# Softmax normalisation of a fused attention and two-MLP kernel: GpSimd keeps the tiles of 320 to 448 keys, DVE and ACT take the others

## The chip, the cores and the metric

One core of a Trainium2 chip runs the kernel. The time is that of the whole launch on the device in microseconds (us), the median of three runs. The engines are PE (TensorE: matrix products and transposes), DVE (VectorE), ACT (ScalarE), POOL (GpSimd) and SP, whose queue issues nearly all DMAs.

## The reference

Causal attention, a gated MLP and an MLP with a rational function follow each other, all in float32:

```python
def _attn_ref(q, k, v):                 # q, k, v: 2 x 12 x 448 x 64
    scores = scale * np.matmul(q, k.transpose(0, 1, 3, 2))
    mask = np.triu(np.ones((seq, seq), dtype=bool), k=1)
    scores = np.where(mask, -1000000000.0, scores)
    scores = scores - np.max(scores, axis=-1, keepdims=True)
    attn = np.exp(scores)
    attn = attn / (np.sum(attn, axis=-1, keepdims=True) + 1e-09)
    return np.matmul(attn, v).astype(np.float32)
...
def _moe_ref(x, w_in, w_out):           # 896 x 768, 768 x 2048, 2048 x 768
    h = x @ w_in
    relu6 = np.clip(h + 3.0, 0.0, 6.0)
    g = h * relu6 / 6.0
    return (g @ w_out).astype(np.float32)
...
def _moe2_ref(x, w_in, w_out, a, b):    # same shapes, g = P(h) / (Q(h) + 1e-6)
```

## The kernel before

The work has two stages. The attention stage takes the 24 heads in 12 pairs, numbered 0 to 11. A pair has seven tiles, r = 0 to 6: 64 queries of each of its two heads against (r + 1) * 64 keys, so tiles of 64 to 448 keys. For each pair PE forms the scores (`a_scores`, L427), DVE adds the mask and takes the row maximum (`a_max`, L439), ACT takes the exponential and its row sums (`a_exp`, L446). In two parts (tiles 6, 5, 0, then 4, 3, 2, 1) the sums get 1e-9 added on ACT or DVE (`a_bias`) and DVE takes the reciprocals (`a_recip`, L462). Then every tile of exponentials is multiplied by its reciprocals: `a_norm`, the normalisation, on GpSimd in this kernel (L470). PE transposes the tiles in four groups (`a_transpose`, L476; the first two groups hold tiles 5, 6 and 0), ACT or DVE moves each group from PSUM to SBUF (`a_move`, tiles `et`, L326 on ACT and L328 on DVE), PE multiplies with v (`a_apply`, L496), and ACT and DVE split the result into a high and a low part (`xh`, L326, and `xl`, L508). The buffers of the exponentials (`e0` to `e6`) exist twice, so pair n + 2 waits for pair n.

The MLP stage follows: 2304 matmuls of 448 columns (L715). Their weights come as float64, are loaded in chunks and are rebuilt by ACT (`full`, `tail`, high part, L610, L616, L326) and DVE (L620, L626, low part, L644). The first chunks are prepared, and the first products formed, while the attention stage still runs.

No engine picks its work at run time. The class `Program` writes out each engine's queue when the kernel is built: it plays the operations through a list of costs, and where two operations could start at the same time it takes the one with the smaller due time. The due time is the operation's place (pair number times `PAIR`) plus an offset for its kind in `DUE`. Where an operation names several engines with a cost each, the planner takes the engine on which it starts first. Each engine then works through its queue strictly in order. `STAY` holds PE back from switching between groups of operations. These numbers are planning figures and not measured ones.

Of the kernel before, what the change touches and what calls it, by code (L numbers as in the profile page):

```python
# [35 lines left out]
class Program:  # L36
# [15 lines left out]

    TILING = {"scores": "quarters", "apply": "columns"}
    DRAIN = 0.16
    STAY = 5.83

    def __init__(self, rings, banks, due):
        self.rings, self.banks, self.due = rings, banks, due
# [2 lines left out]
    def add(self, kind, at, engines, fn, *args, reads=(), writes=(), new=()):  # L61

        self.ops.append((kind, at, engines, fn, args, tuple(reads), tuple(writes), tuple(new)))

    def order(self):
# [44 lines left out]
        while can:  # L112
            best = None
            for n, t in can.items():
# [20 lines left out]
                for e, cost in ops[n][2].items():  # L135
                    mine = max(t[e], free[e], room), due[n] + self.STAY * turn, n, e, cost
                    if best is None or mine < best:
# [46 lines left out]
def c_act(n):  # L184
    return 0.051 + n / 1200


def c_dve(n):
    return 0.068 + n / 960


def c_pool(n):
    return 0.15 + n * 0.0021


def c_pe(n, passes):
    return passes * (0.0025 + n / 2400)

# [5 lines left out]
def c_mm(n, passes):  # L204
# [2 lines left out]


DUE = {
    "load": -89.1,  # L210
    "keep": 0.0,
    "fetch": -20.0,
    "load v": -0.1,
    "norm": 4.2,
    "scores": 10.5,
    "max": -10.7,
    "exp": 31.3,
    "bias": 13.8,
    "reciprocal": -27.8,
    "transpose": -38.3,  # L220
    "move": 7.4,
    "apply": 15.3,
    "x hi": -25.6,
    "x rest": 70.4,
    "constants": -8.8,
    "w load": -84.1,
    "magnitude": -7.3,
    "tail": -30.5,
    "shift": 17.2,
    "sign": -12.6,  # L230
    "w hi": 79.6,
    "w rest": -29.6,
    "product": 0.0,
    "relu": 8.8,
    "gate": 1.1,
# [17 lines left out]
    "out": -3.6,  # L253
    "store": 7.5,
}
PAIR = 5.9


def plan(KM, KF):
# [17 lines left out]
def tile_attention_moe_moe2(  # L277
# [235 lines left out]
    for n in range(len(pairs)):  # L513
        t, last = PAIR * n, n == len(pairs) - 1
        for which in ("kr", "qr"):
            raw = which, n
            add(
                "load", t, {"act" if n == 0 and which == "qr" else "dma": 1.26}, qk_load, which, n,
                writes=[raw], new=[(which, raw)],
            )  # L520
        add(
            "load v", t, {"dma": 0.9}, v_load, n, reads=[("empty", n % VB)], writes=[("v", n)],
            new=[("v", ("v", n))],
        )
        sc = [("sc", n, held) for held in BANKS]
        add(
            "scores", t, {"pe": 1.7}, a_scores, n, reads=[("kr", n), ("qr", n)],
            writes=sc + ["scored"] * last, new=[("s", key) for key in sc],
        )
        for late, r in enumerate(order):  # L530
            w, first, mine = (r + 1) * CP, late == 0, next(held for held in BANKS if r in held)
            add(
                "max", t + late, {"dve": c_dve(w)}, a_max, n, r,
                reads=[("sc", n, mine), "masks"] + [("stat", n)] * (not first)
                + [("m", n, mine[0])] * (r != mine[0]),
                writes=[("e", n, r), ("st", n, r), ("m", n, r)] + [("stat", n)] * first,
                new=[(f"e{r}", ("e", n, r))] + [("stat", ("stat", n))] * first,
            )
            add(
                "exp", t + late, {"act": 0.235 + c_act(w)}, a_exp, n, r, reads=[("stat", n)],  # L540
                writes=[("e", n, r), ("st", n, r)],
            )
        for part, held in enumerate((STRAIGHT, SWAPPED)):
            add(
                "bias", t + 2 * part, {"act": 0.2, "dve": 0.1}, a_bias, n, part,
                reads=[("st", n, r) for r in held] + [("stat", n)], writes=[("r", n, part)],
            )
            add(
                "reciprocal", t + 2 * part, {"dve": 0.15}, a_recip, n, part, reads=[("stat", n)],
                writes=[("r", n, part)],  # L550
            )
            for r in held:
                w = (r + 1) * CP
                add(
                    "norm", t + 2 * part, {"pool": c_pool(w)}, a_norm, n, r,
                    reads=[("r", n, part), ("stat", n)], writes=[("e", n, r)],
                )
        for g, group in enumerate(GROUPS):
            add(
                "transpose", t + g, {"pe": 0.436}, a_transpose, n, g,  # L560
                reads=["masks", ("pads", n % EB)] + [("e", n, r) for r in sorted({r for r, _ in group})],
                writes=[("pt", n, g)], new=[("t", ("pt", n, g))],
            )
            add(
                "move", t + g, {"act": c_act(512), "dve": c_dve(512)}, a_move, n, g,
                reads=[("pt", n, g)], writes=[("et", n, g)], new=[("et", ("et", n, g))],
            )
        for a, gs_ in enumerate(APPLY):
            cols = 1024 * len(gs_) // len(GROUPS)
            add(  # L570
                "apply", t + 2 * a, {"pe": c_pe(cols, 4) + 0.1}, a_apply, n, a,
                reads=[("et", n, g) for g in gs_] + [("v", n)], writes=[("o", n)],
                new=[("o", ("o", n))] if a == 0 else (),
            )
        b, hp = pairs[n]
        add("x hi", t, {"act": c_act(S) + 0.04}, a_hi, n, reads=[("o", n)], writes=[("x", hp, b)])
        add("x rest", t, {"dve": c_dve(S)}, a_lo, n, reads=[("o", n)], writes=[("x", hp, b)])
# [22 lines left out]
    raw, full, tail, split = {}, {}, {}, {}  # L600
# [54 lines left out]

    base = PAIR * len(pairs) + 10

# [208 lines left out]
    t, i, every = base, 0, tuple(range(B))  # L866
# [6 lines left out]
    while i < len(chunks):  # L873

        side = chunks[i][0][0] == 2
        n = 1 if not side else 2 if chunks[i + 2][0][0] == 2 else 3
# [72 lines left out]
```

## Time and profile before

| | |
|---|---|
| median of 3 runs (lowest to highest) | 560.67 us (560.19 to 560.80) |
| the profiled execution: its own time / its span | 560.22 / 558.4 us |
| busy: PE, DVE, ACT, POOL | 538.7, 423.2, 397.9, 82.2 us |
| chain that ended last, by line | 82% MLP matmuls (L715), 11% GpSimd's normalisation (L470) |
| mean granted TensorE clock | 0.991 |

The span goes from the first to the last instruction in the trace; the run's own time holds a little more. Busy time is that in which an engine has an instruction in work. The chain is followed back from the last instruction, at each step to what released it.

### The profile page before, as it was taken

How to read it: one execution, taken by the hardware profiler on the slowest of the kernel's cores; microseconds unless marked ns; L12 is line 12 of the kernel's file. 1: busy time of each engine (PE TensorE's matmuls, PEld its weight loads, DVE VectorE, ACT ScalarE, POOL GpSimd, SP SyncE). 2: the span in 40 equal slices, each digit the busy share in tenths (PEclk: the TensorE clock that was granted, in tenths of full speed). 3: DMA queues.
4: the chain of work that ended last, by engine and by line, in shares of the span. 5: the costliest groups of instructions: out<-in, count | busy, mean ns of one | idle time of the engine just before them, and what ended most of it. 6: DMA issues, size and time to landing. Idle time of an engine off the chain costs nothing.

```text
span 558.4 us, 9410 instructions
## 1 busy us (share of the span) xinstructions
PE 538.7 (96%) x3236; PEld 492.8 (88%) x3236; DVE 423.2 (76%) x925; ACT 397.9 (71%) x882; POOL 82.2 (15%) x104
## 2 busy tenths in 40 slices
PE   6888887999999999999999999999999999999997
PEld 5766766999999999999999999999999999999996
DVE  3588784679999998777777349999989999975420
ACT  5798885579898987776776359788678778855410
POOL 3999978000000000000000000000000000000000
PEclk9699999999999999999999999999999999999999
DMA  5775141147778777777766342234324323336100
GB/s 163 219 202 166 43 119 58 54 146 213 249 253 242 258 231 279 258 252 242 243 236 223 136 137 85 86 94 165 110 85 136 118 86 103 124 112 188 61 33 33
DMA packets 39311, 87.12 MB, mean 156 GB/s; under 512 B 4704, under 2 KB 14688, under 8 KB 39264
## 3 DMA queue, kind: packets, MB, share of 16 engines
q1 hardware_dynamic: 39104, 86.30, 47.9%
q8 instruction: 25, 0.41, 0.3%
q10 hardware_dynamic: 160, 0.23, 0.1%
q14 instruction: 22, 0.18, 0.1%
HBM read 71.18 MB, written 15.34 MB: 155 GB/s over the span
## 4 chain that ended last, share of the span: by engine, by line
PE 85%; POOL 11%; DVE 2%; issue 1%; ACT 1%; POOLq 0%; DVEq 0%
PE bank L715 82%; POOL e L470 11%; DVE e L439 1%; PE bank L476 1%; PE bank L376 1%; PE bank L496 1%; PE bank L427 1%; ACT et L326 0%; DVE et L328 0%; POOLq L945 0%; ACT e L446 0%; ACT o L326 0%; DVE stat L462 0%; ACT tail L616 0%; POOL ident masks.py:199 0%
## 5 line engine op out<-in xcount | busy, mean ns | idle before, releaser
L715 PE MATMUL bank<-yh,w 128*128 128x448 f32 x384 | 112.0, 362 | 0.0
L715 PE MATMUL bank<-rh,w 128*128 128x448 f32 x384 | 97.2, 362 | 0.0
L715 PE MATMUL bank<-xh,w 128*128 128x448 f32 x384 | 93.7, 363 | 0.0
L715 PE MATMUL bank<-ph,w 128*128 128x448 f32 x384 | 92.6, 362 | 0.0
L644 DVE TENSOR_TENSOR w<-full,w 128x384 fp32r<-128x384 f32 x96 | 53.2, 555 | 46.0 <-ACT w L326 45.6
L326 ACT ACTIVATE w<-full 128x384 fp32r<-128x384 f32 x96 | 50.2, 523 | 51.6 <-PE bank L715 50.8
L616 ACT ACTIVATE tail<-raw 128x384 uint32<-128x384 uint8 x128 | 69.4, 554 | 23.0 <-DVE full L620 19.7
L610 ACT ACTIVATE full<-raw 128x384 f32<-128x384 f32 x128 | 68.9, 549 | 20.2 <-DVE w L644 19.1
L620 DVE SCALAR_TENSOR_TENSOR full<-full,tail 128x384 uint32<-128x384 uint32 x128 | 69.7, 555 | 17.3 <-ACT full L610 15.5
L470 POOL TENSOR_SCALAR e<-e,stat 128x448 f32<-128x448 f32 (+6 forms) x84 | 79.5, 971 | 12.2 <-DVE stat L462 8.4
L715 PEld LDWEIGHTS bank<-rh,w 128*128 128x128 f32 x384 | 71.9, 188 | 5.2 <-ACT qy L783 0.3
L715 PEld LDWEIGHTS bank<-yh,w 128*128 128x128 f32 x384 | 71.9, 187 | 5.1 <-DVE p L767 0.5
L715 PEld LDWEIGHTS bank<-ph,w 128*128 128x128 f32 x384 | 72.0, 188 | 4.6
L715 PEld LDWEIGHTS bank<-xh,w 128*128 128x128 f32 x384 | 71.7, 188 | 4.5
L626 DVE SCALAR_TENSOR_TENSOR full<-raw,full 128x384 uint32<-128x384 uint32 x128 | 69.5, 558 | 1.9
L715 PE MATMUL bank<-yl,w 128*128 128x448 f32 x192 | 69.6, 363 | 0.0
L715 PE MATMUL bank<-rl,w 128*128 128x448 f32 x192 | 54.3, 362 | 0.0
L715 PE MATMUL bank<-xl,w 128*128 128x448 f32 x192 | 53.8, 361 | 0.0
L715 PE MATMUL bank<-pl,w 128*128 128x448 f32 x192 | 53.8, 361 | 0.0
L446 ACT ACTIVATE e<-e,stat 128x448 f32<-128x448 f32 (+6 forms) x84 | 41.7, 503 | 7.7 <-DVE stat L439 7.2
L476 PE MATMUL bank<-ident,e 128*128 128x128 f32 x192 | 28.5, 295 | 15.0 <-POOL e L470 15.0
L476 PEld LDWEIGHTS bank<-ident,e 128*128 128x128 f32 x192 | 22.4, 149 | 22.6 <-POOL e L470 22.4
(56 smaller groups left out, 732.9 us busy)
## 6 DMA issues: line engine op xcount, KB each, us to landing
raw<-in_w SPq DMA_DIRECT2D x128, 384.0 KB, 3.5
kept<-ws SPq DMA_DIRECT2D x32, 384.0 KB, 4.1
w<-kept SPq DMA_DIRECT2D x32, 384.0 KB, 3.3
kr<-in_kT SPq DMA_DIRECT2D x24, 112.0 KB, 2.9
out_T<-o SPq DMA_DIRECT2D x12, 224.0 KB, 2.2
qr<-in_qT SPq DMA_DIRECT2D x22, 112.0 KB, 2.9
v<-in_v SPq DMA_DIRECT2D x12, 128.0 KB, 2.8
v<-in_v SPq DMA_DIRECT2D x12, 96.0 KB, 3.0
```

The lines of the kernel that those rows point to most:

```text
L326: e.activation(out, in_, AF.Copy)
L376: e.matmul(bank[banks[0]][:, :P], ident, ident, start=True, stop=True)
L427: e.matmul(tiles["sc", n, r][halves[slot]], q[halves[j], r * CP:w], k[halves[j], :w], start=True, stop=True,)
L446: e.activation(t, t, AF.Exp, bias=stat[:, 0, at_:at_ + 1], scale=-1.0, accum_out=stat[:, 1, at_:at_ + 1],)
L470: e.tensor_scalar(t, t, by, None, ALU.mult)
L476: e.transpose(to[:, x], es[n % EB][r][:, c * P:(c + 1) * P], ident)
L610: e.activation(full[i], high, AF.Copy, scale=TO_F32)
L616: e.activation(tail[i], top, AF.Copy, bias=-31.0 / 64.0, scale=1.0 / 32.0)
L620: e.scalar_tensor_tensor(bits, bits, 3, tail.pop(i), ALU.logical_shift_left, ALU.bitwise_or)
L626: e.scalar_tensor_tensor(bits, raw.pop(i)[:, :, :, 1], 0x80000000, bits, ALU.bitwise_and, ALU.bitwise_or)
L644: e.tensor_tensor(split[i][:, 1], full.pop(i), split[i][:, 0], ALU.subtract)
L715: e.matmul(sums[which, m, b], split[i][:, w, j, :], x, start=k == 0 and n == 0, stop=last and n == 2,)
```

## The change

`a_norm` may now run on several engines. A new function gives the planner the choice: in pairs 1 to 9 the tiles of 320, 384 and 448 keys stay on GpSimd, and the shorter ones may go to DVE, ACT or GpSimd; in pair 0 all go to DVE or ACT; in pairs 10 and 11 the long ones go to DVE or ACT and the short ones to any of the three. `a_norm` itself had both forms of the multiply already. The other edits are numbers of the planner: `STAY`, `PAIR`, two PE costs and a good part of `DUE`.

```diff
-    STAY = 5.83
+    STAY = 2.84
...
+def c_norm(n, r, w):
+    fast = {"dve": 0.07 + w / 960, "act": 0.06 + w / 1200}
+    if 0 < n < 10 and r > 3:
+        return {"pool": 0.25 + w * 0.00252}
+    return fast if n == 0 or r > 3 else {**fast, "pool": 0.25 + w * 0.00252}
+
+
...
-    "norm": 4.2,
-    "scores": 10.5,
...
+    "norm": -71.7,
+    "scores": 73.4,
...
-PAIR = 5.9
+PAIR = 5.6
...
-            "scores", t, {"pe": 1.7}, a_scores, n, reads=[("kr", n), ("qr", n)],
+            "scores", t, {"pe": 1.42}, a_scores, n, reads=[("kr", n), ("qr", n)],
...
-                    "norm", t + 2 * part, {"pool": c_pool(w)}, a_norm, n, r,
+                    "norm", t + 2 * part, c_norm(n, r, w), a_norm, n, r,
```

What the planner makes of it is seen in the queues. Lines of the changed kernel from the tables on stand seven higher than before (the norm is L475 on ACT and L477 elsewhere, the exponential L453). The buffers of pairs 1, 3, ... are e_98 (64 keys) to e_104 (448), those of the even pairs e_91 to e_97; the number after `stat_` tells pairs apart.

First ACT's queue at the start of the program. Before, from the bias add of pair 0 on (pair 0 has stat_196, pair 1 stat_214):

```order
L456 ACTIVATE stat_196<-stat_196 128x3
L446 ACTIVATE e_104,stat_214<-e_104,stat_214 128x448
L446 ACTIVATE e_92,stat_196<-e_92,stat_196 128x128
L446 ACTIVATE e_98,stat_214<-e_98,stat_214 128x64
L446 ACTIVATE e_102,stat_214<-e_102,stat_214 128x320
L446 ACTIVATE e_100,stat_214<-e_100,stat_214 128x192
```

And in the changed kernel, where pair 0 has stat_193:

```order
L463 ACTIVATE stat_193<-stat_193 128x3
L453 ACTIVATE e_104,stat_214<-e_104,stat_214 128x448
L475 ACTIVATE e_97<-e_97,stat_193 128x448
L475 ACTIVATE e_91<-e_91,stat_193 128x64
L453 ACTIVATE e_92,stat_193<-e_92,stat_193 128x128
L453 ACTIVATE e_98,stat_214<-e_98,stat_214 128x64
L453 ACTIVATE e_102,stat_214<-e_102,stat_214 128x320
L333 ACTIVATE et_1_266<-bank_76 128x512
L475 ACTIVATE e_94<-e_94,stat_193 128x256
L475 ACTIVATE e_93<-e_93,stat_193 128x192
```

Four norms of pair 0 now stand between exponentials on ACT; each waits for a reciprocal of DVE. On PE the first transposes of pair 0 moved from behind the scores of three pairs to behind those of two.

Second, GpSimd's queue for one pair, number 9, before:

```order
L470 TENSOR_SCALAR e_104<-e_104,stat_984 128x448
L470 TENSOR_SCALAR e_103<-e_103,stat_984 128x384
L470 TENSOR_SCALAR e_98<-e_98,stat_984 128x64
L470 TENSOR_SCALAR e_102<-e_102,stat_984 128x320
L470 TENSOR_SCALAR e_101<-e_101,stat_984 128x256
L470 TENSOR_SCALAR e_100<-e_100,stat_984 128x192
L470 TENSOR_SCALAR e_99<-e_99,stat_984 128x128
```

And the end of GpSimd's queue in the changed kernel, pairs 9 (stat_970), 10 (stat_1063) and 11 (stat_1139):

```order
L477 TENSOR_SCALAR e_104<-e_104,stat_970 128x448
L477 TENSOR_SCALAR e_103<-e_103,stat_970 128x384
L477 TENSOR_SCALAR e_102<-e_102,stat_970 128x320
L477 TENSOR_SCALAR e_91<-e_91,stat_1063 128x64
L477 TENSOR_SCALAR e_94<-e_94,stat_1063 128x256
L477 TENSOR_SCALAR e_98<-e_98,stat_1139 128x64
L477 TENSOR_SCALAR e_101<-e_101,stat_1139 128x256
```

Seven tiles a pair became three in pairs 1 to 9, none in pair 0 and two each in pairs 10 and 11.

Third, DVE's queue at the end of the attention stage of the changed kernel, behind the last maximum of pair 11:

```order
L627 SCALAR_TENSOR_TENSOR full_1148<-full_1148,tail_993 128x384
L335 COPY et_1_1194<-bank_78 128x512
L633 SCALAR_TENSOR_TENSOR full_1141<-raw_405,full_1141 128x384
L633 SCALAR_TENSOR_TENSOR full_1148<-raw_430,full_1148 128x384
L335 COPY et_2_1225<-bank_76 128x512
L335 COPY et_3_1236<-bank_77 128x512
L469 RECIPROCAL stat_1139<-stat_1139 128x3
L515 TENSOR_TENSOR xl_85<-bank_74,xh_84 128x448
L477 TENSOR_SCALAR e_103<-e_103,stat_1139 128x384
L469 RECIPROCAL stat_1139<-stat_1139 128x4
L477 TENSOR_SCALAR e_102<-e_102,stat_1139 128x320
L477 TENSOR_SCALAR e_99<-e_99,stat_1139 128x128
```

The reciprocals of pair 11 and three of its norms stand here behind moves of pair 10; before, DVE had no norms.

## Rows read from the trace of the kernel before

**Rows 1.** The chain that ended last, in order of time: start us, us, what.
```profile
88.38 6.83 POOL e L470 x7
...
95.25 1.09 PE bank L476 x8
96.34 1.21 PE bank L715 x6
97.55 1.91 PE bank L496 x32
99.46 455.52 PE bank L715 x2274
```

**Rows 2.** Four stretches: busy us and instructions by engine, granted clock, DMA.
```profile
7.97:24.81 16.84, 12.39 (x123) 9.44 (x116) 10.46 (x53) 13.18 (x51) 13.24 (x15) 0.70 0.68 204
24.81:86.45 61.64, 54.09 (x686) 42.93 (x684) 49.28 (x195) 54.60 (x183) 57.51 (x61) 1.00 0.46 131
86.45:96.34 9.89, 6.92 (x73) 5.82 (x70) 3.90 (x8) 5.32 (x11) 8.74 (x10) 1.00 0.25 80
100.00:555.00 455.00, 454.96 (x2273) 425.49 (x2271) 358.89 (x669) 321.81 (x636) 0.00 (x0) 1.00 0.49 161
```

**Rows 3.** Groups by line and shape, 0 to 100 us: xcount, busy us, mean ns.
```profile
L470 POOL TENSOR_SCALAR e<-e,stat 128x448 f32<-128x448 f32 x12 | 16.9, 1407 | 12.2 <-DVE stat L462 8.4 <-DVE stat L439 3.8
...
L470 POOL TENSOR_SCALAR e<-e,stat 128x384 f32<-128x384 f32 x12 | 15.4, 1283 | 0.0
...
L470 POOL TENSOR_SCALAR e<-e,stat 128x320 f32<-128x320 f32 x12 | 13.9, 1154 | 0.0
...
L439 DVE CUSTOM_DVE_ANT_0 e<-bank,mask 128x448 f32<-128x448 f32 x12 | 7.4, 617 | 7.5 <-PE bank L427 7.3
...
L470 POOL TENSOR_SCALAR e<-e,stat 128x64 f32<-128x64 f32 x12 | 6.4, 531 | 0.0
...
L439 DVE CUSTOM_DVE_ANT_0 e<-bank,mask 128x64 f32<-128x64 f32 x12 | 2.5, 210 | 0.0
```

**Rows 4.** Who waited for whom: PE 0 to 100 us; ACT 24.81 to 86.45.
```profile
PE bank L476 <- POOL e L470: 15.0, 15, 3.3
...
ACT et L326 <- PE bank L476: 2.5, 5, 0.9
```

**Rows 5.** ACT in order of time: start us, duration us, instruction.
```profile
11.04 0.19 ACT L456 ACTIVATE stat<-stat 128x3 f32<-128x3 f32 x1
11.14 0.65 ACT L446 ACTIVATE e<-e,stat 128x448 f32<-128x448 f32 x1
...
24.81 0.67 ACT L446 ACTIVATE e<-e,stat 128x448 f32<-128x448 f32 x1
...
55.40 0.39 ACT L446 ACTIVATE e<-e,stat 128x128 f32<-128x128 f32 x1
...
55.78 0.51 ACT L326 ACTIVATE w<-full 128x384 fp32r<-128x384 f32 x1
56.20 0.19 ACT L456 ACTIVATE stat<-stat 128x4 f32<-128x4 f32 x1
56.55 0.60 ACT L326 ACTIVATE et<-bank 128x512 f32<-128x512 f32 x1 [0.16 <-PE bank L476]
57.05 0.52 ACT L326 ACTIVATE w<-full 128x384 fp32r<-128x384 f32 x1
```

**Rows 6.** PE in order of time, merged, at the start and in mid-stage.
```profile
5.90 5.04 PE L427 MATMUL bank<-kr,qr 64*64 64x64 f32 x84
14.25 1.97 PE L476 MATMUL bank<-ident,e 128*128 128x128 f32 x8 [3.31 <-POOL e L470]
...
37.32 1.09 PE L476 MATMUL bank<-ident,e 128*128 128x128 f32 x8 [1.52 <-POOL e L470]
38.34 1.98 PE L496 MATMUL bank<-et,v 128*64 128x128 f32 x32
40.25 1.75 PE L427 MATMUL bank<-kr,qr 64*64 64x64 f32 x28
```

**Rows 7.** Stretches of 1 us: columns as in rows 2, granted clock behind POOL.
```profile
13.00:14.00 1.00, 0.00 (x0) 0.00 (x0) 0.00 (x0) 1.00 (x6) 1.00 (x1) 0.53 0.61 181
22.00:23.00 1.00, 1.00 (x9) 0.54 (x4) 0.00 (x0) 0.50 (x2) 1.00 (x2) 0.50 0.83 247
```

More of the change, by code (lines that the diff above doesn't have):

```diff
@@ L209 @@
 DUE = {
-    "load": -89.1,
+    "load": -66.8,
     "keep": 0.0,
     "fetch": -20.0,
-    "load v": -0.1,
-    "norm": 4.2,
-    "scores": 10.5,
[L216 to L224, printed above, removed]
-    "constants": -8.8,
[L226 to L232, printed above, removed]
+    "load v": -6.2,
+    "norm": -71.7,
+    "scores": 73.4,
+    "max": -32.0,
+    "exp": 10.8,
+    "bias": 4.9,
+    "reciprocal": -29.8,
+    "transpose": -21.5,
+    "move": 6.5,
+    "apply": 23.1,
+    "x hi": 5.2,
+    "x rest": 62.2,
+    "constants": -8.8,
+    "w load": -87.2,
+    "magnitude": 45.8,
+    "tail": -50.0,
+    "shift": -31.3,
+    "sign": -2.7,
+    "w hi": 63.9,
+    "w rest": -7.0,
     "product": 0.0,
@@ L570, in tile_attention_moe_moe2 @@
             add(
-                "apply", t + 2 * a, {"pe": c_pe(cols, 4) + 0.1}, a_apply, n, a,
+                "apply", t + 2 * a, {"pe": c_pe(cols, 4) + 0.08}, a_apply, n, a,
                 reads=[("et", n, g) for g in gs_] + [("v", n)], writes=[("o", n)],
```

## The prediction, made before the changed kernel's time was known

> **What bounds the kernel now.** I read the chain of work that ended last first. From 99.46 us to 554.98 it is one unbroken run of 2274 MLP matmuls, 455.52 / 2274 = 0.2003 us each [rows 1]; between 100 and 555 us TensorE (PE) is busy all the time, and DVE and ACT have room (359 and 322 us of 455) [rows 2]. The end is therefore fixed by the moment at which the last attention transposes are through, plus a known amount of PE work. Call that moment X. Before, X is 96.34 us: GpSimd (POOL) normalises pair 11 from 88.38 to 95.20, eight transposes follow, then six MLP matmuls, the apply of pair 11, and the run [rows 1].
>
> Next, what sets X. A GpSimd tile costs 0.53 us (64 keys) to 1.41 us (448 keys) [rows 3], the seven of a pair the 6.83 us of the chain. From the first exponential of pair 3 (24.81 us [rows 5]) to the last exponential (86.45), GpSimd is busy 57.5 of 61.6 us, ACT 54.6, PE 54.1, DVE 49.3; in the 9.9 us after it GpSimd works 8.7 and ACT and DVE 5.3 and 3.9 [rows 2]. PE's transposes wait 15.0 us for GpSimd [rows 4]. So GpSimd is the bound, but ACT and PE stand close behind it (89% and 88%): that limits what its relief can be worth. Only in the last 9.9 us is there nothing close behind.
>
> **The change, part by part.** *Removed from GpSimd.* Of 84 tiles it keeps 27 (the three long ones of pairs 1 to 9) and gets four short ones (64 and 256 keys of pairs 10 and 11). The three long ones take 1.407 + 1.283 + 1.154 = 3.84 us a pair [rows 3], against the 6.85 us (61.64 / 9) that a pair takes in the middle stretch. It stops being a bound. What is late next is ACT.
>
> *Added to ACT and DVE.* By the order of the changed program ACT gets 29 tiles and DVE 24. The trace has no such multiply on ACT, so I price it by ACT's own instructions from start to start: the 3-column bias add 0.10 us (11.04 to 11.14), the 384-column copy of a weight 0.42 (55.78 to 56.20) [rows 5]. The line through both gives 0.15, 0.205, 0.26, 0.31, 0.42 and 0.47 us for 64, 128, 192, 256, 384 and 448 keys. For a bound above, the whole duration of the copy (0.51, 0.09 more) counts [rows 5]: 0.09 x 29 = 2.6 us in all. Less than the line is excluded by the bias add, which takes its 0.10 us for 3 columns. I take the line, because the instruction after the copy does start 0.09 us before its end.
>
> [...]
>
> *ACT's work, start.* From pair 0's first exponential (7.97 us) to pair 3's (24.81), ACT is busy 13.18 of 16.84 us [rows 2], 3.66 idle. Afterwards this part has six norms more (448, 256, 2 x 192, 2 x 64: 1.60 us), one 128-key exponential (0.38, 55.40 to 55.78 [rows 5]) and one bias add (0.10) less: 14.3 us, so pair 3 starts at 22.3 us if nothing waits, at 26.0 with the old idle time. PE decides between: it does two pairs' scores instead of three before the first transposes. Scores take 1.68 us a pair (84 matmuls, 5.04 us), so PE stops at 9.3 instead of 10.9; the first norms (ACT behind the exponential that starts at 11.14 and takes 0.65, DVE beside it) are done at about 12.3 [rows 5], where GpSimd's let PE start at 14.25 [rows 6]. The gap stays as long, about 3.1 us for 3.3. [...] I take half of the old idle time, 1.8 us: pair 3 at 24.1.
>
> *ACT's work, middle and end.* Counted by the order, from that point to the last norm of pair 11 ACT has, against the old stretch to the last exponential: 23 norms (7 x 0.31 + 7 x 0.205 + 4 x 0.26 + 3 x 0.15 + 0.42 + 0.47 = 6.0), one exponential (0.38), one move of transposed tiles (0.50, 56.55 to 57.05 [rows 5]) and one output copy (taken as 0.44) more, three weight steps (3 x 0.42) and one bias add less: 54.6 + 6.0 = 60.6 us. Old idle time in the stretch: 61.64 - 54.60 = 7.0 us. Of it 2.5 went to moves that waited for transposes [rows 4], which waited for GpSimd. That part should shrink, but new waits come in: a norm on ACT waits for a reciprocal on DVE, and DVE's queue has moves in front of that (pair 11: two of them). [...] I take two thirds of the old idle time, 4.7 us.
>
> *Sum.* 24.1 + 60.6 + 4.7 = 89.4 us for the last norm; 0.04 to the transposes (88.38 + 6.83 to 95.25) and 1.09 for eight [rows 1]: X = 90.5. ACT ends this stretch 3 us later than its last exponential before, yet X comes 5.8 us earlier, since no 6.83 us of GpSimd follow.
>
> *DVE* gets 24 tiles of 200 keys on average; by the nearest row, its maximum over 64 columns in 0.21 us and over 448 in 0.62 [rows 3], one takes 0.35, all 8.5 us. At 49.3 of 61.6 us busy in the middle stretch alone it has 12.3 us free, so I cost that at nothing beyond the waits above. If that cover is gone, the norms of DVE come late by the same amount.
>
> *What is behind X.* The program now has 48 MLP matmuls before the last apply, 30 before; 24 stand ahead of X in both. 90.5 + 24 x 0.2003 + 1.91 = 97.2; 2256 x 0.2003 = 451.9 gives 549.1; the tail of 558.4 - 554.98 = 3.4 gives a span of 552.5. The weights' order changes in a few places later; with DVE and ACT 79% and 71% busy there [rows 2] I cost this at nothing. The load queue sends the first four pairs in the same order, which the start needs. The profiled run took 560.22, 1.8 more than its span, and the median is 0.45 above it: 552.5 + 1.8 + 0.45 = 554.8 us, 1.0% faster.
>
> **The rivals.** *ACT runs through.* If the waits vanish with GpSimd (none at the start, 1 us after it), X = 22.3 + 60.6 + 1.0 + 1.14 = 85.0, and the time is 560.67 - 11.3 = 549.3 us. For it: the old idle time lies mostly behind GpSimd. [...]
>
> *The old gaps stay.* With the idle time of before, 3.66 + 7.04 us, X = 22.3 + 60.6 + 10.7 + 1.14 = 94.7 and the time 559.0. For it: ACT, DVE and PE work in order, each at 88 to 95%, and hand every tile round several times.
>
> *More gaps than before: slower.* The norms stand in the same in-order queues as the exponentials and the moves; a norm that waits for its reciprocal holds every exponential behind it, and these hold the next pair's reciprocals. The place is ACT's queue, pairs 3 to 11. The change loses when idle time on ACT exceeds 96.34 - 1.14 - 22.3 - 60.6 = 12.3 us from pair 0 on; it was 10.7. Half as much again as before, 16 us, gives X = 100.0 and 564.4 us. Against it: GpSimd, which caused much of the old idle time, is out.
>
> **How the numbers follow.** A measurement of this kernel tells about 0.2% (1.1 us) from no change. Forecast, 552 to 558 us: 0.52. ACT runs through, below 552: 0.17. Old gaps stay, 558 to 561.8: 0.20, half of it within 0.2% (above 559.5). Slower: 0.11. So faster 0.79, same 0.10, slower 0.11. The range, 549.5 to 560.3, leaves out about 0.03 below and 0.16 above; the bound on the ACT price (2.6 us) lies inside it.
>
> **What would show it.** Right: GpSimd busy about 38 us instead of 82, gone from the chain's end; ACT 94% busy or so from pair 3 to the last norm; norms on ACT 0.15 to 0.47 us from start to start; the last transposes near 90 us; after them an unbroken run of matmuls at 0.2003. Half clock again in the first 25 us. Wrong: the first exponential of pair 3 far from 24 us, ACT's idle time outside 2 to 10 us, ACT norms at 0.24 us or more for 64 keys, or holes in PE after 97 us (weights late by their new order).

## The result, and the profile after

The changed kernel takes 552.52 us (median of four runs, 552.43 to 553.43), the kernel before, run beside it, 560.43 (560.06 to 560.80). The ratio is 0.9863, with a 95% interval of 0.9845 to 0.9880: 1.4% faster, against 1.0% forecast. The profiled execution took 552.57 us with a span of 550.8.

The chain that ended last in the changed kernel, in order of time (start us, us, what; the rows that answer to [rows 1]):

```profile
33.36 4.78 DMA cb<-in_b
...
84.81 1.91 PE bank L503 x32
86.72 1.90 PE bank L483 x16
88.62 4.82 PE bank L722 x24
93.44 1.91 PE bank L503 x32
95.35 451.96 PE bank L722 x2256
547.31 0.02 issue
547.33 0.55 ACT o L333
```

GpSimd no longer stands ahead of the last transposes. They end at 88.62 us: this is X, 96.34 before. Behind it come the 24 matmuls, the last apply and one unbroken run of 2256 matmuls, and 3.5 us of tail (550.8 - 547.31). Of the gain of 7.9 us X accounts for 7.7 (96.34 - 88.62). A DMA of 128x2 coefficients of the rational function (cb) stands in the chain as well, which nothing of before has.

Stretches of the changed kernel, columns as in [rows 2], [rows 7]: from pair 0's first exponential to pair 3's, from there to the end of pair 11's last norm on ACT, the MLPs, and 1-us stretches at the start (PE has its gap before the first transposes until 12.69):

```profile
8.56:24.01 15.45, 10.95 (x118) 7.82 (x112) 12.01 (x61) 14.40 (x53) 3.82 (x4) 0.89 0.72 204
24.01:87.03 63.02, 59.20 (x745) 47.24 (x741) 53.27 (x212) 60.42 (x207) 32.62 (x28) 1.00 0.43 124
100.00:545.00 445.00, 445.00 (x2224) 416.41 (x2223) 356.98 (x668) 320.02 (x632) 0.00 (x0) 1.00 0.51 164
...
11.00:12.00 1.00, 0.00 (x0) 0.00 (x0) 1.00 (x8) 1.00 (x6) 0.00 (x0) 1.00 0.73 169
...
13.00:14.00 1.00, 0.94 (x9) 0.76 (x8) 0.51 (x4) 1.00 (x7) 0.00 (x0) 1.00 0.65 174
14.00:15.00 1.00, 1.00 (x15) 0.84 (x18) 0.96 (x4) 1.00 (x4) 0.00 (x0) 0.62 0.68 197
15.00:16.00 1.00, 1.00 (x14) 0.71 (x10) 0.32 (x2) 1.00 (x4) 0.00 (x0) 0.50 0.68 186
16.00:17.00 1.00, 1.00 (x12) 0.24 (x5) 0.46 (x2) 1.00 (x5) 0.00 (x0) 0.50 0.56 83
17.00:18.00 1.00, 1.00 (x10) 1.00 (x7) 0.01 (x1) 0.38 (x3) 0.00 (x0) 0.67 0.77 261
18.00:19.00 1.00, 1.00 (x20) 0.80 (x22) 1.00 (x5) 0.57 (x2) 0.00 (x0) 1.00 0.97 382
```

In the middle stretch ACT is busy 60.42 of 63.02 us (96%), PE 59.20, DVE 53.27, GpSimd 32.62; in the MLPs PE has no hole (445.00 of 445). GpSimd's busy time over the whole span is 39.6 us, forecast with 38. ACT idles 2.60 us in the middle stretch, and who waited for whom says that this is a single wait (us in total, times, longest; ACT from 24 to 87 us, PE from 8 to 91):

```profile
ACT cabs L600 <- DMA cb<-in_b: 2.6, 1, 2.6
...
PE bank L483 <- POOL e L477: 2.5, 3, 1.6
```

PE's waits for GpSimd fell from 15.0 us [rows 4] to 2.5. Now the events in order of time (as [rows 5], [rows 6]), first ACT, then PE, DVE and GpSimd:

```profile
30.25 0.34 ACT L475 ACTIVATE e<-e,stat 128x64 f32<-128x64 f32 x1
30.49 0.39 ACT L453 ACTIVATE e<-e,stat 128x128 f32<-128x128 f32 x1
...
35.35 0.20 ACT L453 ACTIVATION_READ_ACCUMULATOR e<-e,stat 128x1 f32 x1
38.16 0.20 ACT L600 ACTIVATE cabs<-cb 128x2 f32<-128x2 f32 x1 [2.60 <-DMA cb<-in_b]
...
85.19 0.76 ACT L475 ACTIVATE e<-e,stat 128x448 f32<-128x448 f32 x1
85.75 0.30 ACT L463 ACTIVATE stat<-stat 128x4 f32<-128x4 f32 x1
...
86.67 0.55 ACT L475 ACTIVATE e<-e,stat 128x192 f32<-128x192 f32 x1
87.01 0.62 ACT L333 ACTIVATE w<-full 128x384 fp32r<-128x384 f32 x1
...
12.69 1.37 PE L483 MATMUL bank<-ident,e 128*128 128x128 f32 x8 [2.81 <-DVE e L477]
...
39.59 0.42 DVE L477 TENSOR_SCALAR e<-e,stat 128x192 f32<-128x192 f32 x1
52.45 0.32 DVE L477 TENSOR_SCALAR e<-e,stat 128x192 f32<-128x192 f32 x1
...
39.37 1.08 POOL L477 TENSOR_SCALAR e<-e,stat 128x320 f32<-128x320 f32 x1 [2.43 <-ACT full L617]
...
51.05 3.81 POOL L477 TENSOR_SCALAR e<-e,stat 128x448 f32<-128x448 f32 x3 [3.50 <-DVE stat L469]
```

A norm on ACT takes 0.24 us for 64 keys (30.25 to 30.49), 0.34 for 192 (86.67 to 87.01) and 0.56 for 448 (85.19 to 85.75) from its start to the next one's: 0.08 to 0.09 above the line of the prediction. The wait for cb holds the exponentials behind it from 35.55 to 38.16.

### The profile page after: what moved, and what is told of

Same layout as the page of the kernel before. It is cut to its first block, busy times and chain, and to the rows that moved or that the text cites. A ratio compares the mean times of both kernels' runs of the same rounds, so it can differ in the third digit from the quotient of the medians.

```text
span 550.8 us, 9402 instructions
## 1 busy us (share of the span) xinstructions
PE 537.6 (98%) x3236; PEld 491.7 (89%) x3236; DVE 429.5 (78%) x953; ACT 404.0 (73%) x907; POOL 39.6 (7%) x51
## 4 chain that ended last, share of the span: by engine, by line
PE 90%; ACT 6%; SPq 1%; DMA 1%; issue 1%; POOL 1%; DVE 0%; POOLq 0%; ACTq 0%
PE bank L722 84%; ACT e L453 3%; PE bank L503 2%; PE bank L483 2%; PE bank L434 2%; DMA cb<-in_b 1%; PE bank L383 1%; ACT e L475 1%; ACT et L333 1%; POOL e L477 0%; SPq L401 0%; ACT xh L333 0%; SPq L407 0%; SPq L406 0%; ACT full L617 0%
## 5 line engine op out<-in xcount | busy, mean ns | idle before, releaser
L453 ACT ACTIVATE e<-e,stat 128x192 f32<-128x192 f32 (+6 forms) x84 | 42.4, 522 | 6.6 <-DVE stat L446 6.6
L477 POOL TENSOR_SCALAR e<-e,stat 128x448 f32<-128x448 f32 (+4 forms) x31 | 36.9, 1201 | 47.1 <-DVE stat L469 42.3
L446 DVE CUSTOM_DVE_ANT_0 e<-bank,mask 128x192 f32<-128x192 f32 (+6 forms) x84 | 31.8, 415 | 8.8 <-PE bank L434 8.6
L722 PEld LDWEIGHTS bank<-yl,w 128*128 128x128 f32 x192 | 36.0, 188 | 2.5
```

What stands on the lines that cost most here:

```text
L446: e.tensor_tensor_reduce(es[n % EB][r][:, :w], tiles.pop(("sc", n, r)), mask[:, S - w:], -0.125, 3.0e38, ALU.add, ALU.min, tiles["stat", n ...
L453: e.activation(t, t, AF.Exp, bias=stat[:, 0, at_:at_ + 1], scale=-1.0, accum_out=stat[:, 1, at_:at_ + 1],)
L477: e.tensor_scalar(t, t, by, None, ALU.mult)
L722: e.matmul(sums[which, m, b], split[i][:, w, j, :], x, start=k == 0 and n == 0, stop=last and n == 2,)
```

## The experiments

All kernels compute the whole result; the two that add work say so. Each ratio is against the kernel before on the same chip, with its 95% interval; X is read in the profiled execution as the end of the last attention transposes.

**1. The coefficients loaded at the start** (the changed kernel). The load of ca and cb goes from its planned place in the load queue to ACT's queue, behind pair 0's q:

```diff
 def qk_load(e, which, n):
...
+        if e is nc.scalar:
+            c_load(e)
...
-    add("constants", 20, {"dma": 0.1}, c_load, writes=["c"])
+    add("constants", 20, {"dma": 0.1}, lambda e: None, writes=["c"])
```

> The changed kernel, but the two small loads of the rational function's coefficients are issued from ACT's queue at the start of the program instead of from the load queue at 32.7 us; every other queue keeps its order. Theory (after GpSimd's relief ACT is the bound of the attention stage, and its only idle time from pair 3 on is the 2.6 us that it waits for these coefficients): the wait goes, the last transposes end 2.2 to 2.6 us earlier, time 549.9 to 550.5 us. Rival (PE, busy 59.2 of 63.0 us in that stretch, is as much of a bound): the wait was cover for PE, the time stays above 551.7 us.

Measured: 549.93 us, ratio 0.9822 (0.9806 to 0.9838), 2.3 us below the changed kernel by the ratios. The early load is worth that; that all of it is the wait is not shown. The wait was 2.6 us in the one trace of the changed kernel, but 0.9 and 1.3 us in those of experiments 5 and 6, where the load stands at the same place of the queue. And the profiled execution of this experiment does not show the gain: it took 551.31 us, where the five lie between 549.55 and 551.66. Two waits of ACT for PE, 2.3 us, stand there where the one for the coefficients stood; ahead of the first, PE itself waits 1.9 us for pair 0's v. ACT's waits, pair 0's first exponential and the chain's end:

```profile
ACT xh L333 <- PE bank L505: 2.3, 2, 1.5
```

```profile
7.55 0.67 ACT L455 ACTIVATE e<-e,stat 128x448 f32<-128x448 f32 x1 [5.55 <-DVE stat L448]
```

```profile
87.36 4.82 PE bank L724 x24
```

X is 87.36 there, 1.26 earlier than in the changed kernel, but 1.01 of this is an earlier start: pair 0's first exponential begins at 7.55 us, in the changed kernel's trace at 8.56. Experiment 11 has the gain in its trace.

**2 and 3. The two halves of the change alone.** The split of the norms with the old table of due times, and the new table with all norms on GpSimd:

```diff
-                    "norm", t + 2 * part, {"pool": c_pool(w)}, a_norm, n, r,
+                    "norm", t + 2 * part, c_norm(n, r, w), a_norm, n, r,
```

(the second is the changed kernel with this line turned back).

> The kernel before with the new split of the normalisation alone; due times, STAY, PAIR and the costs of scores and apply stay as before. Theory (the gain is GpSimd's work leaving the chain, the numbers only fit the queues to it): GpSimd is no longer at the end of the chain, 553 to 557 us. Rival (the new numbers make the gain): 559 us or more.

> The changed kernel with its due times, STAY, PAIR and PE costs, but all 84 tiles normalised on GpSimd as before. Theory: GpSimd still needs 6.83 us a pair and sets the end, 559 to 563 us. Rival (the numbers make the gain): 556 us or less.

Measured: the split alone 558.67 us, 0.9972 (0.9961 to 0.9982), between what the theory and the rival said; the numbers alone 561.61, 1.0026 (1.0015 to 1.0037), as the theory had it. So one half gives 0.28%, the other costs 0.26%, and together they give 1.4%. With the numbers alone the chain ends as before, behind seven GpSimd norms:

```profile
88.55 6.82 POOL e L477 x7
95.41 1.09 PE bank L483 x8
```

With the split alone GpSimd is out of the way, but X is 94.5: pair 3's first exponential comes at 29.67 us instead of 24.01, and from there on the work takes as long as in the changed kernel (64.8 us to X, against 64.6). That exponential, and PE where it stands at the start, in order of time:

```profile
29.67 0.67 ACT L453 ACTIVATE e<-e,stat 128x448 f32<-128x448 f32 x1
...
15.60 1.75 PE L434 MATMUL bank<-kr,qr 64*64 64x64 f32 x28
23.02 3.68 PE L503 MATMUL bank<-et,v 128*64 128x128 f32 x32 [5.68 <-ACT tail L623]
```

The first apply starts 5.68 us after the scores. The releaser named is the last event by the profile; the v of pair 0, which that apply reads, was issued at 18.89 and 19.58 us in the load queue.

**4. The split for pairs 10 and 11 alone**, old table:

```diff
+    if n < 10:
+        return {"pool": c_pool(w)}
```

> The kernel before with the new split for pairs 10 and 11 alone; pairs 0 to 9 stay on GpSimd, all numbers as before. Theory (the gain lies in the 6.83 us in which GpSimd works alone behind the last exponential; in the middle ACT is as slow as GpSimd was): most of the gain of the changed kernel, 554 to 556.5 us. Rival (the gain is made pair by pair in the middle): 558.5 us or more.

Measured: 556.83 us, 0.9942 (0.9928 to 0.9955), just above the theory's range. Taking the 6.83 us of GpSimd from the end [rows 1] is worth 0.6% by itself, under half of the gain, and more than the split of all pairs is with this table.

**5 and 6. How near ACT and DVE are to the bound.** Work that nothing reads is added to the changed kernel, once a pair from pair 3 on, on ACT or on DVE:

```diff
 def a_exp(e, n, r):
+        if n > 2 and r == 3:
+            e.activation(junk, mask[:, :384], AF.Copy)
...
 def a_max(e, n, r):
+        if n > 2 and r == 3:
+            e.tensor_tensor(junk, mask[:, :384], mask[:, 64:], ALU.mult)
```

> The changed kernel with one more copy of 384 columns into a scratch tile on ACT in each of the pairs 3 to 11, 0.42 us each from start to start, 3.8 us in all; nothing reads it and all orders stay. Theory (ACT is the bound): the two copies ahead of the wait for the coefficients are hidden in it, the other seven delay the end by 2.9 us, time 555.0 to 556.0 us. Rival (PE is the bound, ACT has room): under 1 us more, below 553.6 us.

> The changed kernel with one more product of two 384-column operands into a scratch tile on DVE in each of the pairs 3 to 11, about 0.48 us each, 4.3 us in all. Theory (ACT is the bound, DVE has 9.8 us free of 63 from pair 3 on): under 1.3 us more, below 553.9 us. Rival (DVE's reciprocals and moves are on the path as much as ACT's work): 3 us or more, 555.5 us or above.

Measured: nine copies more on ACT, 3.8 us of work, 554.75 us, 0.9899 (0.9886 to 0.9912): 2.2 us more by the medians. The wait for cb was 0.9 us in that trace and 2.6 without the copies; most of the difference is that it ended 1.5 us earlier there (36.66 us for 38.16), so how much added work it hid is not shown. Nine products more on DVE, about 4.3 us, 553.30, 0.9870 (0.9857 to 0.9882): 0.8 us, and the interval holds the changed kernel's ratio. So added work on ACT costs over half of itself and added work on DVE little, as the theory had it, ACT's price a little under its range.

**7 and 8. ACT relieved of the norms.** Both start from experiment 1. First the planner gets DVE and GpSimd alone for the norms after pair 0 (the long ones of pairs 1 to 9 stay on GpSimd), and makes new queues. Then the queues stay, and the 21 norms that ACT has from pair 3 on are issued on DVE where they stand:

```diff
-    fast = {"dve": 0.07 + w / 960, "act": 0.06 + w / 1200}
+    dve, pool = {"dve": 0.08 + w / 1850}, {"pool": 0.25 + w * 0.00252}
...
 def a_norm(e, n, r):
+        if n > 2:
+            e = nc.vector if e is nc.scalar else e
```

> [...] Theory (ACT is the bound): ACT loses some 6 us of norms, the end comes earlier until PE is the bound, 546.5 to 549 us. Rival (PE is already the bound once the coefficients are early): no better than with the early coefficients alone, 550 us or more.

> The changed kernel with the early coefficients, and the 21 norms that ACT has from pair 3 on are issued on DVE instead, at the same place of the plan; PE, GpSimd and the load queue keep their order. ACT's norms take 0.24 to 0.56 us from start to start in the trace of the changed kernel, 21 of them some 7 us; DVE gets some 6 us more. Theory (with the early coefficients ACT is still the bound of the attention stage): 546 to 548.8 us, until PE or DVE is the bound. Rival (no engine is alone the bound: DVE's longer queue delays its reciprocals and moves by what ACT saves): 549.5 us or more.

Measured: 555.84 us, 0.9918 (0.9905 to 0.9931), and 551.96, 0.9858 (0.9837 to 0.9879). The theory fell in both: experiment 1 alone took 549.93. The first is no test of ACT alone: its new queues wait elsewhere (PE's waits for GpSimd are 8.2 us, against 2.5). The second is one. ACT is busy 4.0 us less (56.43 of 62.39 us from 23.61 to 86.00), yet X is 87.36, as in the trace of experiment 1 (0.7 us less if both are counted from pair 0's first exponential). ACT's waits:

```profile
ACT e L455 <- DVE stat L448: 2.7, 7, 0.8
ACT xh L333 <- PE bank L507: 1.2, 1, 1.2
ACT tail L627 <- DVE full L631: 0.8, 1, 0.8
ACT et L333 <- PE bank L487: 0.6, 2, 0.4
```

What ACT gains it waits for: DVE has 59.23 of the 62.39 us to do, PE 58.97. So with ACT's norms gone the others hold the end where it was: ACT is the bound of the changed kernel by a small distance only.

**9 and 10. Whether late loads are what the old table costs the split.** To experiment 2, first pair 0's v from ACT's queue at the start, then pair 1's v and the coefficients as well:

```diff
+        if e is nc.scalar:
+            v_load(e, 0)
...
+            v_load(e, 1)
+            c_load(e)
```

> The split alone with the old numbers, but pair 0's v is loaded from ACT's queue at the start of the program instead of from the load queue at 18.9 us; every other order stays as in the split alone. Theory (the new numbers were worth so much because they put that load ahead: with the old ones PE waits 5.7 us for it at 17 to 23 us, and TensorE then runs at half clock to 27 us): the wait goes, 4 to 5.5 us off the 558.7 us of the split alone, 553.2 to 554.7 us. Rival (the wait only covers other waits that the old order has in the same place): 557.5 us or more.

> The numbers of before with the split, as in the run with pair 0's v from ACT's queue, and now also pair 1's v and the coefficients from that queue, so that the waits of 3.7 us for the coefficients and 2.5 us for pair 1's v have no cause left; all orders on the engines stay. Theory (the old numbers cost the split what their late loads cost): 553 to 556 us, the first exponential of pair 3 at 24 to 26 us. Rival (the old order of work on the engines, norms and moves behind each other in the start, holds pair 3 back whatever the loads do): 557.5 us or more, pair 3's first exponential after 27.5, and other waits of the same sum in place of the loads'.

Measured: 558.62 us, 0.9971 (0.9958 to 0.9985), and 557.88, 0.9950 (0.9933 to 0.9967). The theory fell twice: pair 3's first exponential still comes at 28.35 and 29.61 us:

```profile
28.35 0.66 ACT L455 ACTIVATE e<-e,stat 128x448 f32<-128x448 f32 x1
```

```profile
29.61 0.66 ACT L457 ACTIVATE e<-e,stat 128x448 f32<-128x448 f32 x1
```

With the v there, the next loads are late (of the first kernel, among its waits):

```profile
DVE cneg L599 <- DMA ca<-in_a: 3.7, 1, 3.7
ACT tail L625 <- DMA raw<-in_w: 2.5, 2, 2.0
```

With those there too, others stand in their place (second kernel, 15 to 32 us):

```profile
ACT tail L627 <- DMA raw<-in_w: 3.3, 2, 1.7
PE bank L487 <- DVE et L335: 1.8, 1, 1.8
PE bank L487 <- POOL e L481: 1.8, 1, 1.8
PE bank L487 <- ACT et L333: 1.7, 1, 1.7
```

The loads of v and of the coefficients are not what costs the split its gain under the old table. Nor is it TensorE's clock alone: from 18 to 30 us a mean of 0.72 was granted in experiment 2, in experiment 9 the full 1.00 (first row experiment 2, second experiment 9), and pair 3 came only 1.3 us earlier.

```profile
18.00:30.00 12.00, 6.98 (x56) 6.03 (x57) 5.92 (x22) 8.27 (x28) 7.44 (x6) 0.72 0.88 262
```

```profile
18.00:30.00 12.00, 5.16 (x54) 4.18 (x52) 8.54 (x31) 9.51 (x32) 7.45 (x6) 1.00 0.87 252
```

Either the order on the engines does, or the loads of weights, for which ACT waits 3.3 us ahead of moves that PE needs; no run here separates these two.

**11. The v of pair 0 and the coefficients early**, in the changed kernel (experiment 1, with the `v_load(e, 0)` of the diff above).

> The changed kernel with the coefficients from ACT's queue at the start, as in the first experiment, and pair 0's v from there too, ahead of them. In that experiment PE's first apply still waited 1.9 us for this v. Theory (the start is a chain: what the first apply gains reaches pair 3's exponentials and X): 0.8 to 1.9 us less than the kernel with the coefficients alone, 548.0 to 549.1 us. Rival (PE and DVE are as near as ACT, and the wait turns into another, as when the norms left ACT): within 0.6 us of it, 549.3 to 550.5.

Measured: 549.46 us, 0.9807 (0.9788 to 0.9826), the lowest of all, and within the interval of experiment 1: the rival held. From pair 3's first exponential to the last norm it takes 60.94 us (23.48 to 84.42), 2.1 less than the changed kernel. That stretch, ACT's only wait in it, and X:

```profile
23.48:84.42 60.94, 57.65 (x745) 47.01 (x740) 53.10 (x211) 60.40 (x207) 32.50 (x28) 1.00 0.44 130
```

```profile
ACT xh L333 <- PE bank L506: 0.5, 1, 0.5
```

```profile
86.03 4.82 PE bank L725 x24
```

PE's wait for a v did not go, it moved to pair 1's (1.7 us, at 29.89).

## Why the prediction was right, step by step

**What bounds the kernel, and the tail behind X: shown.** PE's run after X was predicted with 451.9 us and took 451.96; 24 matmuls and the apply took 6.73 for 6.7. No hole opened after 97 us. X was predicted at 90.5 and came at 88.62. That is 1.9 of the 2.3 us by which the time (552.52) lies below its forecast (554.8); most of the rest is the step from the profiled execution to the median, put at +0.45 us, which was -0.05. Experiment 3 shows the old end of the chain when GpSimd keeps its tiles, experiment 4 the gain when only that end is cut.

**ACT's work: right as a sum, by two errors of opposite sign.** Predicted 60.6 us from pair 3 to the last norm, measured 60.42. The term that was too small is the norm on ACT, 0.09 us in each: the 23 norms of this stretch cost 8.0 us (7 x 0.40 + 7 x 0.29 + 4 x 0.34 + 3 x 0.24 + 0.50 + 0.56, the other widths read likewise), not 6.0. That is the upper bound of the prediction, and one of its signs of being wrong (64 keys at 0.24) did come. With that bound (2.6 us for 29 norms) the sum of the prediction is 557.4 us; the price holds and the time does not, because of the next term and of the idle time. The step that failed was to carry the 0.42 us of the 384-column weight copy over to the norm of equal width, which takes 0.50. A nearer row stood in the trace of before: ACT's exponential reads a column of `stat` as the norm does, which the copy doesn't, and took the norm's 0.24 us for 64 keys from start to start (8.64 to 8.88):

```profile
8.64 0.33 ACT L446 ACTIVATE e<-e,stat 128x64 f32<-128x64 f32 x1
8.88 0.19 ACT L446 ACTIVATION_READ_ACCUMULATOR e<-e,stat 128x1 f32 x1
```

That this operand is what costs the 0.09 us no run here tests.

The term that was too large is the old work. Without the norms and the small net of other instructions (-0.04), 60.42 leaves 52.5 us for what the prediction took as 54.60. The 2.1 us are for the larger part ends of instructions with nothing behind them: the bias add takes 0.10 us where the next instruction follows at once, and counts its full 0.19 where ACT then waits [rows 5]. Each idle gap of ACT so adds some 0.1 us to the busy time, as an estimate from these rows. The trace of before has 14 such gaps in this stretch, the changed kernel's has one: that is 1.3 of the 2.1 us. The other 0.8 us stay open.

**ACT's idle time: too large, and in another place.** Predicted 1.8 us at the start and 4.7 after, a half and two thirds of the old idle time by the author's estimate; measured 1.05 (15.45 - 14.40) and 2.60. The many small waits for reciprocals and moves, to which the prediction gave two thirds of the old idle time, did not come. The 2.60 us are one wait for the coefficients, which the prediction didn't name. In the kernel before the same load cost ACT 0.8 us. Loading it early is worth 2.3 us (experiment 1). X came 1.9 us before its forecast: 2.1 by this term, 0.1 by the start and 0.2 by the work, less 0.5, since sixteen transposes end the stretch (1.59 us from ACT's last norm to X) and not eight (1.13).

**The start: right in its parts, its time in part by luck.** Pair 3's first exponential was predicted at 24.1 and came at 24.01. But pair 0's began at 8.56 us in this trace, 0.59 later than the prediction's 7.97, and the stretch between them was 15.45 us long, not 16.1; the two nearly cancel. The gap of PE was predicted with 3.1 us, and was 2.81. The half clock came, but for three to four microseconds instead of nine or more [rows 7]: granted 0.62 between 14 and 15 us, 0.50 until 17, 1.00 from 18. Experiments 2, 9 and 10 show that this part decides: with the same split and the old table, pair 3 comes 4.3 to 5.7 us later and X 5.3 to 5.9. The prediction took "the load queue sends the first four pairs in the same order" as enough; the table moved more than the order of those loads.

**DVE's norms cost nothing: nearly.** The 24 took 9.2 us by their durations, for 8.5 predicted. Experiment 6 prices a further 4.3 us on DVE at 0.8; but with ACT relieved (experiment 8), DVE's and PE's work is next (59.23 and 58.97 us of 62.39), so its cover is thinner than the 12.3 us of before suggested.

**The rivals.** "ACT runs through" (549.3) did not happen with this change, in the main because of the late loads; experiment 11, in which ACT waits 0.5 us from pair 3 on, gives 549.46, with X at 86.03 where the rival had 85.0. "The old gaps stay" is what the split without the new table does (558.67 for 559.0), though its gaps lie at the start. "More gaps: slower" did not come.

## What to carry to other kernels

When the bound leaves an engine that fills 93% of a stretch, list the engines behind it and add their work from start to start by shape: a busy time that is taken from a stretch with many waits holds the ends of instructions too (the bias add 0.19 us for 0.10 here). Then look in the in-order queues for the small constants and loads that used to hide behind the old bound: here moving two tiny DMAs was worth 2.3 us of 10.2. A split of work and the table that orders it are to be judged together: apart they gave 0.28% and -0.26%, together 1.4%.

## What the runs showed of the hardware that was not expected

- A DMA of 128x2 coefficients was 4.78 us in the chain, from its issue at 33.36 us to just before ACT's start at 38.16. From issue to landing the same load took 4.4 us in the trace of before and 5.2 in that of experiment 2.
- DVE's multiply of 192 keys took 0.32 us at 52.45 and 0.42 at 39.59, where it started 0.22 us into a GpSimd norm of 1.08. It was through well before that norm (40.01 for 40.45); at 52.45 GpSimd had norms in work too (three from 51.05 to 54.86). What sets the two times apart is not shown.
- The granted clock stayed at 1.00 through PE's gap of 2.81 us, which ended at 12.69, and fell with PE busy, between 14 and 15 us. Before, it fell in the gap itself (0.53 between 13 and 14 us [rows 7]).
